# One kernel on one core: the first 166 words of a hand-written issue order replaced by 164 others

## Chip, cores and metric

One core of a Trainium2 chip runs the whole program. The metric is the device time of one execution in microseconds. Lower is better. The profile is that of one execution; engines are named PE (matrix products), DVE, ACT and POOL (element-wise work) and SP (whose queue only issues DMAs here; ACT's queue issues a few as well).

## What is computed

A conditioned block: six vectors come from `silu(c) @ w_mod`, and a linear attention and a gated MLP with a product over the positions are each put behind a layer norm that these vectors scale and shift.

```python
mod = (_silu(c) @ w_mod).reshape(1, 6, 1, 448)
sa, ca, ga, sb, cb, gb = ...
h = _layernorm(x) * (1 + ca) + sa
x = x + ga * A(h)          # q, k, v = h @ wqkv; 16 heads of 28
                           # phi_q, phi_k = [softmax(p), softmax(-p)] with p = q @ w_phi, k @ w_phi
                           # o = phi_q @ (phi_k^T v) / (phi_q . sum phi_k); o @ wo
h = _layernorm(x) * (1 + cb) + sb
x = x + gb * B(h)          # z = gelu(h @ w_in); z1 * (w_sp @ layernorm(z2) + b_sp) @ w_out
```

x is 2048 x 448, wqkv is 448 x 1344, w_sp is 2048 x 2048, all in bf16.

## The kernel before

The 2048 rows of x are 16 tiles of 128 rows. The 448 columns are four chunks of 112, so that a chunk and one row of ones (113 rows) fit the partitions; that row carries the shift of the layer norm. The program is a table, ORDER, that is read word by word. A word is a step of the function fast_path with its arguments, behind `@` the bank of the accumulator memory that it writes (`A0` to `A2` and `C` are pairs of banks), behind `/` the engine (V is DVE, S is ACT, G is POOL, Y is SP). There is no planner at run time: each engine runs its own steps in the order of the table, and a step waits for its inputs and for the bank or buffer that it overwrites. A DMA is issued in its place in the queue of SP or ACT; eight DMAs may be under way, and a ninth waits for the landing of the one whose semaphore it reuses.

The change touches the ramp, the part of the table ahead of the word `kE:4`. Its steps are these:

- `ld:` loads (L653 to L684). `wk`, `wq`, `wv` are the three parts of wqkv; `x0`, `x1` one tile of x each, `x2` two tiles, `x3`, `x4`, `x5` four each; `c`; `phi`; `wsa`, `wca`, `wsb`, `wcb`, `wmga`, `wmgb` the parts of w_mod; `wo`, `win0`, `win1` and others later.
- `du:n` (L732): n products of zeros with zeros, read by nobody.
- `ct`, `ce:1` to `ce:4` (L743 to L756): c as a column and its silu; `scb` copies it for `gr` (L938), which makes the gates ga and gb.
- `FTk`, `FTq` (L822) transpose the key and query weights on PE, in two halves; `ETk`, `ETq` (L826, L828) copy the result out. `bd` (L759) spreads w_phi into blocks. `PFk:m`, `PFq:m` (L838) fold w_phi into chunk m of the weights and `EPk`, `EPq` copy that into Wk and Wq.
- `csA`, `ccA` (L767) make the columns of sa and ca, `esA`, `ecA` (L774, L771) bring them into Ga and ca1.
- `SHk`, `SHq`, `SHv` (L781): the shift row of each weight, as a product of Ga with the unscaled weight. `SCk:m`, `SCq:m`, `SCv:m` (L799, L801) then scale chunk m; m = 0 takes its rows from the shift product.
- `l1s:i`, `l1e`, `l1r` (L845 to L853): mean and deviation of tile i; `l1a:i` (L856) writes the normalized tile to xpad. Tiles 0 to 3 are transposed to hT by PE (`X:i`, L869) and copied out by `XE:i`; later pairs go by a DMA transpose (`T1:a,b`, L861).
- `kM:i`, `vM:i` (L879, L887): k and v of tile i. `kE`, `kF` (L882) are the exponentials, `vC` (L890) the copy of v, `kS`, `kR`, `kP` (L893 to L900) the softmax normalization, `kA` (L910) the sum of phi_k^T v over the tiles. `qM`, `qE`, `qF` (L927, L932) do the same for q.
- `m1` to `m6`, `tbl`: constants, and the load of ACT's table.

In the table before, the query weights are loaded, transposed and folded first; PE makes SHv, SHk, SHq one after another, and then the products of v for tiles 0 and 1.

Of the kernel before, what the change touches and what calls it, by code (L numbers as in the profile page):

```python
# [490 lines left out]
kF:5 kE:6 l1s:14 kF:6 qM:2@A1 qE:2 qF:2 kA:0@A0 l1s:15 l1e:12,16/G l1r:12,16 l1a:14/G l1a:12/G l1a:13/G kS:3 T1:8,10 kR:3 kP:3/V kF:7 ld:wmgb/Y T1:12,14
kS:4 kR:4 l1a:15/G T1:14,16 kS:5 kR:5 kA:1@A0 kA:2@A0 kA:3@A0 vM:5@5 vC:5 vC:7 kP:4/V kP:5/G kE:7 kS:7 W:0,4 ld:win0/Y wos:1/G vC:6 kM:10@3 W:0,5 kS:6
ld:wout/Y vM:11@2 vM:4@5 vC:4 ccB@7 W:0,0 ld:bsp/Y ecB kM:9@4 kF:9 kE:9 kA:4@A0 kR:7 csB@5 esB W:0,3 kM:8@7 kF:8 kR:6 kE:8 W:0,6 kP:7/V kM:11@4 kF:11 kS:9
kS:8 kP:6/G kA:5@A0 vM:9@6 vC:9 vM:8@7 kR:8 kP:8/V kR:9 kM:12@5 kA:6@A0 kA:7@A0 kE:11 kS:11 vC:8 kF:10 kE:10 kS:10 kR:10 wos:0/G kP:9/G kR:11 kP:11/G
kP:10/V kF:12 vC:11 kE:12 kS:12 kR:12 kA:8@A0 kP:12/G kM:13@3 kF:13 vM:12@2 kM:14@4 kE:14 kF:14 kE:13 kS:13 kR:13 vC:12 vM:10@5 vC:10 kM:15@6 kF:15 kE:15
kS:14 kR:14 vM:14@7 gr:1@2 kA:9@A0 kA:10@A0 kA:11@A0 vC:14 vM:13@5 vC:13 kA:12@A0 vM:15@3 vC:15 kP:13/G kS:15 kP:14/V kR:15 kP:15/V kA:13@A0 kA:14@A0
kA:15@A0 wos:2/V ge:1 qM:3@C qE:3 KV:1 KV:0 nM:0@A1 nX:0 wts:0/V nC:0 nM:1@A2 nX:1 nC:1 nS:0 wts:1/G YB@0 YE wos:3/G nV:0 qF:3 nT:0 nA:0/G T2:0,1 SHw:2@1
SCw:0,2/S SCw:3,0/S qM:4@C qE:4 nT:1 nA:1/G SHw:3@2 SCw:0,3/V SCw:3,1/G nM:3@A2 SCw:1,1/S wts:5/V nX:3 nC:3 nM:2@A0 nX:2 nC:2 nS:1 nV:1 nT:3 nA:3/G qF:4
qM:5@A1 qE:5 qF:5 SCw:1,0/G nM:4@C nX:4 nM:5@A2 nX:5 T2:1,2 wN:1@3 SCw:2,1/S wR:1/S wQ:1/S nT:2 nA:2/V wN:0@2 wR:0/S wQ:0/S nC:4 nC:5 qM:6@A0 nS:2 nV:2
nT:5 nA:5/G SCw:0,0/V nM:6@A2 nT:4 nA:4/V nM:7@A1 lA:0,2/V lB:0,2/V T2:2,4 wN:2@7 lC:0,2/V lD:0,2/G l2r:0,2 T2:4,6 qE:6 l2a:1/G T3:1,2 nX:7 nX:6 qF:6  # L500
l2a:0/G T3:0,1 wR:2/S wQ:2/S nC:7 nC:6 nS:3 nV:3 wM:3@6 wR:3/V lA:2,4/G lB:2,4/G wQ:3/S qM:7@A0 qF:7 lC:2,4/G qE:7 lD:2,4/G l2r:2,4 l2a:3/G l2a:2/G nT:7
nT:6 nA:6/V nA:7/V T2:6,8 nM:8@A1 SCw:2,0/S T3:2,4 wM:4@6 wR:4/V W:1,1 wM:5@7 wR:5/V lA:4,6/G lB:4,6/G nM:9@A0 nX:9 nC:9 nX:8 nC:8 nS:4 nV:4 nT:8 nA:8/G
W:1,4 zM:1@A2 nT:9 nA:9/G T2:8,10 gt zG:1 zM:0@C zG:0 wM:7@3 wQ:4/S zQ:1/S wQ:5/V lC:4,6/G lD:4,6/G zA:0,2/G zB:0,2/G l2r:4,6 wM:6@2 wR:6/V wQ:6/S wR:7/V
W:1,0 zQ:0/V zC:0,2/G lA:6,8/G nM:11@A0 nX:11 nC:11 yM:0,1@5 W:0,1 yG:0,1 yM:0,0@4 wQ:7/V nM:10@A1 nX:10 nC:10 nS:5 yG:0,0 zD:0,2/G l2a:4/V l2a:5/V T3:4,6
nV:5 zM:2@C zG:2 lB:6,8/G lC:6,8/G zW:0,2 lD:6,8/G nT:11 nA:11/G zM:3@A2 zG:3 nT:10 zQ:2/S nA:10/V T2:10,12 l2r:6,8 wM:9@6 wR:9/V wM:8@7 wR:8/V l2a:6/G
nM:12@A2 nX:12 nC:12 zA:2,4/G lA:8,10/G lB:8,10/G nM:13@A1 nX:13 nC:13 nS:6 nV:6 nT:13 nA:13/V zQ:3/S yM:0,6@0 yG:0,6 yM:0,5@6 wQ:9/S l2a:7/G T3:6,8 W:0,2
W:1,2 zB:2,4/V zC:2,4/G zD:2,4/G zN:0/G yM:0,4@7 yG:0,4 wQ:8/S yG:0,5 lC:8,10/V lD:8,10/V nT:12 nA:12/G zM:4@A0 zG:4 wM:11@2 wR:11/V wQ:11/S wM:10@3
wR:10/V wQ:10/S lA:10,12/V l2r:8,10 nM:15@A2 nX:15 lB:10,12/V lC:10,12/G nM:14@A0 nX:14 lD:10,12/G l2r:10,12 zW:2,4 l2a:9/V nC:14 nC:15 nS:7 nV:7 nT:15
T2:12,14 nT:14 zN:1/V zM:5@C zG:5 nA:14/V zA:4,6/V l2a:8/G zN:2/G T3:8,10 zQ:4/S zN:3/V tT:1,2,4/V yM:0,3@3 l2a:11/G yG:0,3 W:1,6 wts:4/V l2a:10/V nA:15/V
T2:14,16 yM:1,1@2 zB:4,6/G zQ:5/S zC:4,6/G zD:4,6/G zW:4,6 T3:10,12 yM:1,3@6 yM:1,4@7 yG:1,4 zM:7@A2 zG:7 zQ:7/S yM:1,2@3 yG:1,3 zN:5/G zM:6@A0 zG:6 zQ:6/S  # L510
yM:0,2@5 yG:0,2 W:0,7 wM:13@7 yM:1,5@4 yG:1,2 yG:1,5 wR:13/V wQ:13/V zN:4/V wts:2/G zA:6,8/G zB:6,8/G zC:6,8/G zD:6,8/V zW:6,8 zN:6/G yM:1,0@1 wM:12@0
wR:12/V wQ:12/V yG:1,0 lA:12,14/V lB:12,14/G lC:12,14/G lD:12,14/V l2r:12,14 l2a:13/G l2a:12/G T3:12,14 W:1,7 zM:9@C zG:9 zQ:9/S zM:8@A2 wM:15@1 zG:8
wR:15/V wQ:15/S zQ:8/S wM:14@7 zA:8,10/V wR:14/V zB:8,10/V lA:14,16/G lB:14,16/V wQ:14/V lC:14,16/G lD:14,16/G l2r:14,16 yM:2,6@3 zM:11@A2 zG:11 zQ:11/V
yM:2,2@1 yG:2,2 zM:10@C yM:2,0@0 yG:2,6 zG:10 zQ:10/S yG:2,0 yG:1,1 zC:8,10/G tT:1,4,6/V zA:10,12/G l2a:15/V zM:12@A2 zN:7/V zG:12 l2a:14/V zB:10,12/V
T3:14,16 W:1,3 zM:13@C zD:8,10/G zW:8,10 zN:8/G zC:10,12/V zD:10,12/G yM:2,3@3 zN:9/V zW:10,12 zN:11/V zN:10/V tT:2,2,4/V zG:13 zA:12,14/V yM:1,6@1 yG:2,3
zQ:13/S zB:12,14/V zQ:12/S zC:12,14/G zD:12,14/V zW:12,14 zN:12/V zN:13/V tT:3,4,6/V tT:3,2,4/V wts:6/V tT:1,0,2/V yM:3,4@0 yG:3,4 zM:15@C zM:14@A1
yM:3,3@4 zG:15 W:1,5 sS:0,1,1/V zG:14 zA:14,16/G zQ:14/S yM:3,1@5 zB:14,16/G zQ:15/S yG:3,1 yG:1,6 zC:14,16/V zD:14,16/G zW:14,16 zN:15/V zN:14/V
tT:1,6,8/V tT:2,6,8/V yM:2,4@7 tT:2,4,6/V yG:2,4 tT:3,6,8/V yM:3,2@6 yM:3,6@0 yM:3,0@2 yG:3,0 tT:3,0,2/V tT:2,0,2/V yM:2,5@3 yM:3,5@5 yG:2,5 sS:0,1,0/V
yM:2,1@1 sS:0,2,1/V W:2,7 tT:4,2,4/V yG:2,1 tT:4,6,8/V yG:3,2 guard yG:3,5 W:2,3 W:2,4 yG:3,6 sS:0,2,0/V gM:0,6@3 W:2,2 gG:0,6 W:2,5 gM:1,6@7 sS:0,3,0/V
pM:0,0,1@6 pc:0,0 pb:0,0 pM:0,1,1@5 pM:0,0,2@6 gG:1,6 cA:0,0,11 cX:0,0,11/G tT:4,4,6/V pc:0,1 sS:0,3,1/V pM:0,2,1@1 pM:0,1,2@5 W:2,6 W:2,0 pb:0,1 pc:0,2  # L520
pM:0,2,2@1 pM:0,0,6@0 uB:0,0 pM:0,0,7@2 yG:3,3 uA:0,0 uW:0,0 pM:0,1,6@4 tT:4,0,2/G pM:0,0,4@2 pM:0,1,7@3 sS:0,4,0/V uB:0,1 uA:0,1 wts:3/V uW:0,1 pM:0,2,6@7
pb:0,2 uB:0,2 pM:0,1,4@3 cA:0,1,11 uA:0,2 pM:0,2,7@6 uW:0,2 W:3,4 W:2,1 W:3,6 W:3,0 cA:0,2,11 sS:0,4,1/V cA:0,0,21 pM:0,0,5@0 cA:0,1,21 cX:0,2,11/G
cX:0,0,21/G cX:0,1,21/G pM:0,2,4@6 W:3,7 W:3,2 W:3,5 cA:0,0,22 cX:0,0,22/V W:3,1 pM:0,1,5@4 cA:0,1,22 pM:0,0,3@0 cA:0,2,21 cX:0,2,21/V pM:0,2,5@7 cA:0,0,12
cA:0,2,22 cX:0,0,12/V cX:0,1,22/V pM:0,1,3@4 pM:0,2,3@7 sS:1,3,0/V cA:0,2,12 guard2@3 pM:1,0,1@1 pc:1,0 pM:1,1,1@2 cX:0,2,12/V cA:0,1,12 cX:0,1,12/V
sS:1,3,1/V pc:1,1 pM:1,0,2@1 cA:1,0,11 pM:1,2,1@5 pc:1,2 pM:1,1,2@2 guard3 sS:1,1,1/V sS:1,2,1/V cX:0,1,11/G cA:1,1,11 pM:1,2,2@5 oM:0,0,7@3 W:3,3
sS:1,1,0/V oE:0 oM:1,0,7@6 oE:1 oD:1/Y oD:0/Y cX:0,2,22/G pb:1,1 oM:2,0,7@0 oE:2 oM:3,0,7@4 oE:3 sS:1,2,0/V sS:1,4,0/V oM:4,0,7@3 oM:5,0,7@6 oM:6,0,7@0
# [777 lines left out]
```

## Time and profile before

| | |
|---|---|
| runs | 250.62 us median of 3 (250.29 to 251.96) |
| the profiled execution | 250.58 us, of which the span from first to last instruction is 248.7 |
| PE busy | 238.8 us of the span |
| DVE, POOL, ACT busy | 184.6, 124.9, 116.8 us |
| first product of x with a weight | 16.04 us from the start |
| granted clock of PE, mean of the span | 0.998 |

The page of the profile gives shares of the span. Views beside it list the waits (who waited for whom), the chain of work that ended last, the instructions in order of time, and, for chosen stretches, the busy time of each engine with the granted clock, the DMA share and GB/s. Times in these views count from the start of the span. A line number is that of the kernel's source.

### The profile page before, as it was taken

The page shows a single profiled execution, that of the slowest core. Times are in us where ns is not written, and L with a number is a line of the kernel's source. Part 1 is how long each engine was busy: PE and PEld are TensorE (multiplying, and loading weights), DVE is VectorE, ACT ScalarE, POOL GpSimd, SP SyncE. Part 2 cuts the span into 40 slices and gives each one's busy share as a digit, 9 for nine tenths or more (in the row PEclk, how much of TensorE's full clock was granted, in tenths as well). Part 3 has the DMA queues.
Part 4 walks back from the last instruction along what each step waited for, and adds up shares of the span by engine and source line. Part 5 has one row for each costly group of instructions (what it writes and reads, how often), then busy time and mean ns, then how long its engine had stood idle before and what let it go on. Part 6 is the DMA issues. An engine that isn't in the chain of part 4 may idle for free.

```text
span 248.7 us, 4193 instructions
## 1 busy us (share of the span) xinstructions
PE 238.8 (96%) x1511; PEld 126.3 (51%) x1519; DVE 184.6 (74%) x374; ACT 116.8 (47%) x233; POOL 124.9 (50%) x170
## 2 busy tenths in 40 slices
...
GB/s 164 263 297 165 176 242 216 190 191 0 61 68 128 171 147 150 86 129 58 108 45 4 137 158 1 3 0 151 193 35 3 37 55 55 3 0 3 18 78 67
DMA packets 68800, 25.23 MB, mean 101 GB/s; under 512 B 58401, under 2 KB 68642, under 8 KB 68770
## 3 DMA queue, kind: packets, MB, share of 16 engines
...
q8 instruction: 14, 0.23, 0.4%
...
## 4 chain that ended last, share of the span: by engine, by line
PE 90%; DMA 5%; ACT 1%; DVE 1%; issue 0%; SPq 0%; DVEq 0%
PE f_psum L1146 29%; PE f_psum L1066 10%; PE f_psum L1036 9%; PE f_psum L1095 8%; PE f_psum L927 6%; PE f_psum L1082 6%; PE f_psum L879 5%; PE f_psum L887 5%; PE f_psum L990 4%; DMA f_wv<-in_A_wqkv_dram 3%; PE f_psum L910 3%; PE f_psum L955 3%; DMA f_wq_raw<-in_A_wqkv_dram 2%; PE f_psum L781 1%; ACT f_Eq L932 1%; PE f_psum L786 1%
## 5 line engine op out<-in xcount | busy, mean ns | idle before, releaser
L1146 PEld LDWEIGHTS <-f_z2n 128*128 128x128 bf16 x192 | 18.7, 98 | 22.4
L1146 PE MATMUL f_psum<-f_wsp,f_z2n 128*128 128x512 bf16 x119 | 27.2, 379 | 0.1
L1198 POOL TENSOR_TENSOR f_z1T<-f_gb,f_z1T 128x512 bf16<-128x512 f32 x6 | 8.4, 1414 | 35.8 <-DVE f_gb L1173 35.8
L1036 PE MATMUL f_psum<-f_win,f_hT 112*128 112x448 bf16 (+1 forms) x128 | 26.2, 352 | 0.0
L1066 PE MATMUL f_psum<-f_hT,f_win 112*128 112x512 bf16 x112 | 26.0, 379 | 0.0
L1146 PE MATMUL f_psum<-f_hT,f_Eq 128*128 128x512 bf16 x92 | 22.3, 379 | 0.2
L1166 ACT COPY f_Eq<-f_psum 128x512 f32<-128x512 f32 x4 | 2.3, 586 | 38.6 <-PE f_psum L1146 38.6
L1095 PE MATMUL f_psum<-f_wout,f_z1T 128*128 128x448 bf16 x105 | 20.4, 352 | 0.0
L1069 ACT ACTIVATE f_z1T<-f_psum,f_yb 128x512 bf16<-128x512 f32 x28 | 18.1, 682 | 1.8 <-PE f_psum L1066 1.8
L1036 PEld LDWEIGHTS <-f_hT 112*128 112x128 bf16 (+1 forms) x128 | 12.3, 97 | 11.7
L932 ACT ACTIVATE f_Eq<-f_psum 112x1024 bf16<-112x1024 f32 x16 | 16.1, 1033 | 3.7 <-PE f_psum L927 3.5
L893 DVE TENSOR_REDUCE f_ksum<-f_E 128x32 f32<-128x896 bf16 x16 | 16.7, 1062 | 1.5 <-ACT f_E L882 1.5
L974 DVE TENSOR_TENSOR f_t<-f_psum,f_w 128x896 bf16<-128x896 f32 x16 | 16.9, 1086 | 0.5
L1066 PEld LDWEIGHTS <-f_win 112*128 112x128 bf16 x112 | 10.9, 98 | 12.3
L882 ACT ACTIVATE f_E<-f_psum 128x448 bf16<-128x448 f32 x32 | 15.7, 567 | 2.8 <-PE f_psum L879 2.2
L1040 ACT ACTIVATE f_z2g<-f_psum 128x896 bf16<-128x896 f32 x16 | 14.6, 914 | 4.8 <-PE f_psum L1036 4.0
L900 POOL TENSOR_TENSOR f_phik<-f_E,f_kr 128x896 bf16<-128x896 bf16 x8 | 14.5, 1813 | 4.5 <-DVE f_kr L897 3.8
L1111 DVE TENSOR_TENSOR f_xpad<-f_psum,f_x 128x448 bf16<-128x448 f32 x15 | 9.2, 621 | 8.6 <-PE f_psum L1095 8.6
L1146 PEld LDWEIGHTS <-f_Eq 128*128 128x128 bf16 x96 | 9.4, 98 | 11.3
L927 PE MATMUL f_psum<-f_hT,f_Wq 113*128 113x512 bf16 (+1 forms) x64 | 15.0, 378 | 0.0
L1095 PEld LDWEIGHTS <-f_z1T 128*128 128x128 bf16 x105 | 10.2, 98 | 9.4
L887 PE MATMUL f_psum<-f_wv,f_hT 113*128 113x448 bf16 (+1 forms) x64 | 14.1, 352 | 0.0
...
## 6 DMA issues: line engine op xcount, KB each, us to landing
...
f_wm<-in_w_mod_dram SPq DMA_DIRECT2D x4, 406.0 KB, 6.6
f_win<-in_B_w_in_dram SPq DMA_DIRECT2D x2, 784.0 KB, 6.6
f_x<-in_A_x_dram SPq DMA_DIRECT2D x3, 448.0 KB, 9.5
f_wmg<-in_w_mod_dram SPq DMA_DIRECT2D x2, 392.0 KB, 7.2
f_wout<-in_B_w_out_dram SPq DMA_DIRECT2D x1, 784.0 KB, 9.4
...
f_wq_raw<-in_A_wqkv_dram ACTq DMA_DIRECT2D x1, 392.0 KB, 4.8
```

Source lines behind the costliest of these rows:

```text
L882: nc.scalar.activation(out=Er[i % NR][:, s, :], in_=ps["k" + str(i)][:, 0, 0:D], func=ACT.Exp, scale=1.0 - 2.0 * s)
L887: nc.tensor.matmul(t[:, 0, 0:D], lhsT=hT[0:KR[m], i, m, :], rhs=wv[0:KR[m], m, :], start=(m == 0), stop=(m == KC - 1))
L893: nc.vector.tensor_reduce(out=ksum[:, i], in_=Er[i % NR][:].rearrange("p s (c f h) -> p (s c) h f", c=4, h=HP), axis=AX.X, op=ALU.add)
L927: nc.tensor.matmul(t[:, u, :], lhsT=Wq[0:KR[m], m, cc * CB:cc * CB + P], rhs=hT[0:KR[m], 4 * st:4 * st + 4, m, :], start=(m == 0), stop=(m ...
L932: nc.scalar.activation(out=Eq[st // 2][0:CB, 2 * c2:2 * c2 + 2, s, (st % 2) * 512:(st % 2 + 1) * 512], in_=ps["q" + str(n)][0:CB, :, :], f ...
L974: nc.vector.tensor_tensor(out=tr[i % 2][:], in0=numv(i)[:, :, :, 0:DH], in1=wr[i // 2 % 2][:, i % 2].unsqueeze(3).to_broadcast([P, 2, H, D ...
L1036: nc.tensor.matmul(t[:, hf, 0:D], lhsT=hT[0:KR[m], i, m, :], rhs=win_s[0:KR[m], m, FH + hf * D:FH + (hf + 1) * D], start=(m == 0), stop=(m ...
L1066: nc.tensor.matmul(t[:, 0, :], lhsT=win_s[0:CB, m, fc * P:(fc + 1) * P], rhs=hT[0:CB, 4 * st:4 * st + 4, m, :], start=(m == 0), stop=(m == ...
L1069: nc.scalar.activation(out=stage_b()["z1T"][:, fc, st * 512:(st + 1) * 512], in_=ps["y%d_%d" % (st, fc)][:, 0, :], func=ACT.Gelu_apprx_tan ...
L1082: nc.tensor.matmul(g[:, 0, 0:b - a], lhsT=later["z2n"][:, s_, fc * P:(fc + 1) * P], rhs=wspT[t][:, s_, a:b], start=(s_ == 0), stop=(s_ == ...
L1095: nc.tensor.matmul(ps["o" + str(t)][:, 0, 0:D], lhsT=later["z1T"][:, fc, t * P:(t + 1) * P], rhs=wout_s[:, fc, :], start=(fc == 0), stop=( ...
L1146: nc.tensor.matmul(t[:, 0, :], lhsT=b[:, j, f * P:(f + 1) * P], rhs=a[:, j, :], start=(PSTART[k] and j == 0), stop=(j == NH - 1), skip_gro ...
```

## The change

Only the table is edited. From `kE:4` on, its 811 words are the same in the same order (they are wrapped into other lines). Ahead of that:

- wk comes by ACT's queue and wq by SP's; x0 is ahead of x1; x2 is behind wsa and wca; wmga and wcb are ahead of x5; wo is behind `T1:4,6`.
- The key weights are transposed and folded ahead of the query weights.
- SHk and SHq are ahead of SHv; the products of k for tiles 0 and 1 are ahead of those of v.
- 18 products of zeros instead of 24, all at the start.
- Banks are given out anew, and some copies and scalings change their engine.

```diff
-ld:x1/Y m2b/G m5 m1/V du:3@1 du:3@5 du:3@7 du:3@3 du:3@0 ld:wq/S ld:c/S tbl m2a/G ld:wk/Y ld:phi/Y l1s:1 bd/V l1e:1,2/G l1r:1,2 ld:x0/Y l1s:0 l1e:0,1/G m4
-FTq:0@5 ETq:0/S ct@1 ce:1 FTq:1@3 ETq:1/V FTk:0@7 ETk:0/S l1r:0,1 l1a:0/G FTk:1@6 ETk:1/S ce:2 ce:3 ce:4 scb du:3@0 m3 du:3@2 ld:x2/Y PFq:3@3 PFq:1@7
-EPq:1/S du:3@0 ld:wsa/Y PFq:0@4 m6 l1a:1/V X:1@0 PFq:2@1 l1s:2 l1s:3 l1e:2,4/V l1r:2,4 EPq:0/S PFk:0@5 EPk:0/S csA@6 esA PFk:1@2 EPq:3/S PFk:2@7 EPk:2/V
-EPk:1/S PFk:3@4 EPk:3/S X:0@5 XE:0/V ld:wca/Y ccA@6 ecA EPq:2/S ld:wv/Y SHv@3 SCv:1/S SCv:0/S SCv:2/V SHk@7 SCk:0/S SCk:1/S SHq@6 XE:1/V l1a:2/G X:2@0
-XE:2/S ld:x3/Y l1a:3/G X:3@4 SCk:2/V SCv:3/V vM:0@5 XE:3/S vM:1@1 SCk:3/V vC:1 SCq:3/S vC:0 kM:0@7 vM:2@0 vC:2 kE:0 kF:0 kM:1@2 kM:2@5 ld:x4/Y SCq:2/S
-SCq:1/V ld:wo/Y ld:x5/Y SCq:0/S l1s:5 l1s:4 l1s:7 kM:3@4 ld:wcb/Y kF:1 l1s:6 l1e:4,8/V l1r:4,8 l1a:7/G kF:2 l1a:6/G vM:3@7 vC:3 kE:1 kE:2 kF:3 l1s:9 l1s:11
-kE:3 l1s:8 l1a:5/G qM:0@A0 l1s:10 l1a:4/V qE:0 l1e:8,12/G l1r:8,12 l1a:11/G qM:1@A1 qE:1 l1s:13 l1s:12 qF:1 kS:0 ld:wmga/Y gr:0@5 kS:1 T1:6,8 vM:6@6 vM:7@4
-kM:7@7 ge:0 qF:0 kR:0 l1a:9/G kR:1 l1a:8/G l1a:10/G T1:4,6 kM:4@2 kP:1/G kP:0/V
+m5 m1/V ld:wk/S m2a/G m2b/G du:3@3 du:3@1 du:3@2 du:3@4 ld:x0/Y l1s:0 l1e:0,1/G du:3@5 du:3@7 ld:c/S ct@3 FTk:0@6 tbl ce:1 ce:2 ce:3 ce:4 scb FTk:1@2
+l1r:0,1 l1a:0/G m3 ld:wq/Y FTq:0@3 ld:x1/Y FTq:1@0 ETk:0/V ld:phi/Y ld:wsa/Y bd/V ETk:1/S PFk:1@6 PFk:3@7 PFk:0@1 ETq:1/V ETq:0/S EPk:3/S PFk:2@4 X:0@3
+EPk:0/S EPk:1/V PFq:3@0 EPq:3/S EPk:2/S PFq:2@5 l1s:1 l1e:1,2/G csA@7 esA PFq:1@1 EPq:1/S EPq:2/V PFq:0@2 EPq:0/S ld:wca/Y ccA@6 ld:x2/Y XE:0/S l1r:1,2
+SHk@0 ecA SCk:1/S SCk:0/S l1s:2 SCk:2/V l1s:3 l1a:1/G m4 SCk:3/V l1e:2,4/G l1r:2,4 ld:wv/Y SHq@5 SCq:1/V X:1@7 XE:1/S SCq:2/V ld:x3/Y SHv@3 SCv:2/S SCv:0/S
+SCv:1/V SCv:3/V SCq:0/S kM:0@2 kF:0 l1s:4 kM:1@0 kF:1 l1s:5 l1s:6 l1s:7 vM:1@3 l1a:3/G X:3@7 XE:3/S kE:0 SCq:3/S kS:0 l1a:2/G vM:0@4 X:2@6 XE:2/S kE:1 vC:0
+vC:1 kM:3@5 kF:3 kE:3 l1e:4,8/G l1r:4,8 l1a:6/G vM:3@1 vC:3 l1a:4/G ld:x4/Y l1s:8 kM:2@6 l1a:5/G l1a:7/V m6 l1s:9 ld:wmga/Y gr:0@0 l1s:10 l1s:11 l1e:8,12/G
+l1r:8,12 l1a:9/G l1a:11/G l1a:8/G kR:0 kF:2 ld:wcb/Y ld:x5/Y l1s:12 vM:2@7 qM:1@A2 vC:2 ge:0 qM:0@A1 qF:1 kE:2 qE:1 T1:6,8 kM:7@7 vM:6@6 qF:0 T1:4,6 kM:4@1
+kP:0/V kS:1 l1s:13 vM:7@4 kR:1 ld:wo/Y l1a:10/V qE:0 kP:1/G
 kE:4 ld:win1/Y kS:2 kR:2 kF:4 T1:10,12 kM:5@0 kE:5 ld:wsb/Y kP:2/G kM:6@5
...
```

More of the change, by code (lines that the diff above doesn't have):

```diff
@@ L491 @@
[L491 to L526, printed above, removed]
```

50 lines of the change are left out of this document (43 added, 7 removed).

## The prediction, as it went on record

> **What bounds the kernel now.** I read the page first. Its first two lines say who works:
>
> ```profile
> span 248.7 us, 4193 instructions
> PE 238.8 (96%) x1511; PEld 126.3 (51%) x1519; DVE 184.6 (74%) x374; ACT 116.8 (47%) x233; POOL 124.9 (50%) x170
> ```
>
> PE is the bound; only its late start can be won. So the next view is the chain that ended last, over the first 31 us (start, length, what):
>
> ```profile
> 0.72 4.83 DMA f_wq_raw<-in_A_wqkv_dram
> 5.55 0.02 issue
> 5.57 0.32 SPq L660
> 5.89 0.04 issue
> 5.93 7.33 DMA f_wv<-in_A_wqkv_dram
> 13.26 0.04 issue
> 13.30 2.44 PE f_psum L781 x12
> ```
>
> Until 13.26 the chain is DMA: the value weights wv land then. From 13.30 on it is PE: first the three shift products SHv, SHk, SHq (L781, four matmuls each, 2.44 us together), then two transposed tiles (X:2, X:3) and the products of x. PE's waits (who waited for whom, total, times, longest), in 13.2 to 60 us and in 60 to 70 us:
>
> ```profile
> PE f_psum L781 <- DMA f_wv<-in_A_wqkv_dram: 0.6, 1, 0.6
> ```
>
> ```profile
> PE f_psum L955 <- DVE f_t L974: 0.7, 1, 0.7
> PE f_psum L988 <- ACT f_Eq L932: 0.4, 1, 0.4
> ```
>
> The first is the wait for wv itself. So behind wv PE is not short of work for 50 us, and every microsecond of PE work that is moved from behind 13.3 to ahead of it shortens the run by one.
>
> **The change, part 1: the loads.** The words behind `kE:4` are the same. In the ramp, wk goes to ACT's queue and wq to SP's second place; x0 leads; x2 moves behind wsa and wca; wo goes from ahead of x5 to behind `T1:4,6`; wmga and wcb go ahead of x5. The issues and their times to landing (last column):
>
> ```profile
> f_wk_raw<-in_A_wqkv_dram SPq DMA_DIRECT2D x1, 392.0 KB, 5.7
> f_x<-in_A_x_dram SPq DMA_DIRECT2D x1, 224.0 KB, 5.7
> 3.18 0.47 SPq L660 DMA_DIRECT2D f_wm<-in_w_mod_dram  x1
> f_wm<-in_w_mod_dram SPq DMA_DIRECT2D x1, 406.0 KB, 7.0
> f_wm<-in_w_mod_dram SPq DMA_DIRECT2D x1, 406.0 KB, 6.2
> f_wv<-in_A_wqkv_dram SPq DMA_DIRECT2D x1, 392.0 KB, 7.3
> 3.00:21.00 18.00, 15.89 (x172) 11.05 (x171) 13.12 (x41) 12.79 (x26) 8.12 (x22) 1.00 1.12 272
> ```
>
> Landings: wq 5.55 (the chain's first row), wk 5.7 after an issue at 1.2, so 6.9, wsa 3.18+7.0 = 10.2, wca 5.57+6.2 = 11.8, wv 13.26: in order of issue, while the DMA runs full (share 1.12, 272 GB/s from 3 to 21 us). Order and bytes then set a landing. wk and wq change places: wk 5.55, wq 6.9. Ahead of wv stand the same loads as before (wk, wq, c, phi, x0, x1, wsa, wca, x2), so **wv lands at 13.26 again**, ±0.3. But wsa and wca gain the 224 KB of x2: 0.23 MB at 272 GB/s is 0.84 us, so by rate wca lands at 10.9 and wsa at 9.2 (without the gain: 11.8, 10.2), and x2 just after wca, 11.8 (at worst 12.4). The ninth load waits in both orders: SP's issue at 5.57 came with the landing of the ACT queue's first load, and now that is wk in the same place.
>
> **Part 2: the work ahead of wv.** Prices (starts of successive rows give the spacing):
>
> ```profile
> 7.12 0.63 DVE L759 TENSOR_TENSOR f_BD<-f_phi,f_bmask 112x448 bf16<-112x448 bf16 x1 [2.37 <-DMA f_phi<-in_A_w_phi_dram]
> 10.52 0.37 PE L838 MATMUL f_psum<-f_BD,f_wTq 112*112 112x112 bf16 x4
> 10.73 0.37 PE L838 MATMUL f_psum<-f_BD,f_wTk 112*112 112x112 bf16 x4
> 14.07 0.92 PE L781 MATMUL f_psum<-f_Wk,f_Ga 112*128 112x448 bf16 x4
> 14.83 0.92 PE L781 MATMUL f_psum<-f_Wq,f_Ga 112*128 112x448 bf16 x4
> 15.83 0.62 DVE L845 BATCH_NORM_STATS2 f_st<-f_x 128x6 f32<-128x448 bf16 x1
> 21.70 1.35 SPq L861 DMA_TRANSPOSE f_hT<-f_xpad  x1
> 16.10:24.60 8.50, 7.93 (x18) 1.00 0.86 194
> ```
>
> A fold group costs PE 0.21, a shift product 0.76; the last row (ACT alone) gives 7.93/18 = 0.44 for one ACT operation; the rows of 15.83 and 21.70 are the start of the statistics of tiles 4 to 7 and the issue of T1:6,8. Walking the new order: wk at 5.55, so `ct`, `FTk` at 5.6 to 7.0; `FTq` waits for wq and for bank 3, which `ce:4` frees, 7.2 to 8.1. `bd` is behind `ETk:0` on DVE, done at 8.3; the four `PFk` then take 0.84, to 9.2; `X:0`, `PFq:3`, `PFq:2` to 9.8; `csA` (wsa is there) to 10.2; `PFq:1`, `PFq:0` to 10.7; `ccA` waits for wca, 10.9 to 11.4. ACT copies behind them one at a time, the last (`EPq:0`) at 11.6. So **SHk runs at 11.4 and SHq at 12.1, to 12.9, ahead of wv**; `X:1` fits to 13.1. At 13.3 only SHv is left. Before, SHv was followed by SHk, SHq and two X; now by two X, further down. Gain: 2 x 0.76 = **1.52 us**. If wca gains nothing (11.8), SHk and SHq end at 13.7 and PE is 0.4 late: gain 1.1. If `PFk` came a further 1.5 us late as well: gain 0. The other way, wv 0.3 early with SHq done in time: 1.8.
>
> The dummies fall from 24 matmuls to 18. They cost nothing before 13.3 and save nothing; what they keep up is the clock:
>
> ```profile
> 1.23 3.38 PE L732 MATMUL f_psum<-f_zero 128*128 128x256 bf16 x15 [1.23 <-DVE f_zero L693]
> 5.00:6.00 1.00, 0.41 (x8) 0.41 (x8) 0.00 (x0) 0.00 (x0) 0.86 (x3) 1.00 1.19 249
> 244.00:245.00 1.00, 0.02 (x1) 0.00 (x0) 0.39 (x1) 0.00 (x0) 0.00 (x0) 1.00 0.59 183
> 247.60:248.70 1.10, 0.00 (x0) 0.00 (x0) 0.00 (x0) 0.00 (x0) 0.00 (x0) 0.51 0.05 15
> ```
>
> The first 15 took 3.38 us, so 18 end at 5.3. The granted clock stayed 1.00 in a microsecond with PE 41% busy, and fell to 0.51 at 247.6, some 3.5 us after PE's last matmul at 244.0. My walk has no gap of PE over 0.5 us (5.3 to 5.6, 10.7 to 10.9), so I cost the lost dummies at nothing; without that cover, one stretch as long as that, 3.5 us, at half pace costs 1.7. The Trainium skill, TensorE: Matmul & The Clock Gate, Part 1, speaks against taking fillers out: the clock returns to half after an idle window of about 3.4 us, in windows that run freely. The fall at 247.6 agrees with it; by that rule too the gaps here are too short, and the sum is unchanged.
>
> **Part 3: from 13.3 to where the orders meet.** PE has the same products in both (8 of k and v, `gr:0`, two qM). New order: SHv to 14.06, `kM:0`, `kM:1`, `vM:1`, `X:3`, `vM:0`, `X:2`, `kM:3`, `vM:3`, `kM:2`, `gr:0`, `vM:2`, `qM:1`, `qM:0`. Each needs ACT to be in time. With 0.45 to 0.55 for each of ACT's operations, SCv:0 is done at 15.4 (`vM:1` asks at 15.6), XE:3 at 17.35 (`kM:3` at 17.5), XE:2 at 18.85 (`kM:2` at 19.05), kE:3 at 21.1 (`qM:1` at 21.35). All fit, with 0.15 to 0.25 to spare, and late hand-overs share one ACT backlog instead of adding up. DVE has l1s:2 and l1s:3 ahead of SCk:3, which is then done at 13.9 (with x2 at 12.4: 14.5, wanted at 14.6). The statistics of tiles 4 to 7 follow at 14.9; with the old 5.9 us from there T1:6,8 is issued at 20.8, which leaves it 4.0 us to land for `kM:7` at 24.8. I take the whole 1.5 here; the lower bound is a 10% slower ACT over these 13 us, 1.3 us, which leaves 0.2. Above zero nothing more can come, since PE is full.
>
> **Part 4: behind the meeting point.** The moved loads can bite here:
>
> ```profile
> 9.47 1.72 SPq L669 DMA_DIRECT2D f_x<-in_A_x_dram  x1
> f_x<-in_A_x_dram SPq DMA_DIRECT2D x1, 448.0 KB, 11.5
> 24.46 0.58 SPq L653 DMA_DIRECT2D f_win<-in_B_w_in_dram  x1
> f_win<-in_B_w_in_dram SPq DMA_DIRECT2D x1, 784.0 KB, 6.9
> 27.02 1.23 SPq L861 DMA_TRANSPOSE f_hT<-f_xpad  x1
> f_hT<-f_xpad SPq DMA_TRANSPOSE x1, 5.6
> 21.00:23.00 2.00, 2.00 (x12) 0.96 (x11) 1.90 (x6) 2.00 (x6) 1.83 (x4) 1.00 0.22 54
> 24.00:27.00 3.00, 3.00 (x17) 1.44 (x15) 3.00 (x6) 2.93 (x5) 2.89 (x6) 1.00 0.77 134
> 35.07 0.93 PE L879 MATMUL f_psum<-f_Wk,f_hT 113*128 113x448 bf16 x4
> ```
>
> x5 landed at 21.0; with wmga and wcb (798 KB) in place of wo (392) ahead of it, 0.42 MB at 272 GB/s, it lands at 22.5. DVE reaches `l1s:12` at 22.4, so no more than some tenths are lost there, with `kP:0`, `kS:1`, `kR:1` and `l1a:10` behind it. `l1a:10` releases T1:10,12: 26.3 instead of 27.0. wo is now between T1:4,6 and win1, so T1:10,12 is behind 0.40 MB more: 1.5 us at 272 GB/s, less the 0.7 by which it and win1 start earlier. Its landing is not told; the queue puts it between win1 (24.46+6.9 = 31.4) and the next transpose (the row of 5.6, issued 1.9 us after T1:10,12, so 34.5). It is next behind win1, so I take 31.7. `kM:10` reads it at 35.07, in the new order at 33.5. Landing near 32.5 costs nothing; at the late bound (34.5+0.8) it costs 1.8, the gain and a little. I take nothing. Everything later waits for progress and not for a clock time, and moves by the same 1.5.
>
> **Sum.** The profiled execution took 250.58 us (span 248.7 and 1.9 around it), the median of the runs is 250.62. 250.58 - 1.5 = **249.1 us**, own range 248.5 to 249.8.
>
> **Rivals.**
> *Hand-overs eat the gain* (wca no earlier, or ACT the bound from 14 to 27 us): gain 0 to 0.7, 249.9 to 250.6. For it: ACT is busy for 7.93 of 8.5 us, and the margins are 0.15 to 0.25. Against: behind 13.3 ACT has seven scalings and hT copies instead of nine, since SCk:0 and SCk:1 now run ahead of wv. Chance 0.17.
>
> *Slower: tiles 10 and 11 of hT arrive late.* The place is `kM:10`, where PE stands with all that is behind it. It decides from a landing of 35.0 on (33.5 and the gain of 1.5). If wo moves at the 134 GB/s of 24 to 27 us, its 0.40 MB takes 3.0 us: from the late bound 34.5 + 3.0 - 0.7 = 36.8, a stall of 3.3, 252.4. T1:8,10 and two more follow in the same queue; each late pair adds up to an equal step, so 251 to 255, with 253 in the middle. For it: wo, win1 and four transposes now stand in one queue in 23 to 35 us, and that stretch moved only half the full rate. Against: the DMA had room just before (share 0.22 in 21 to 23), and the first taken value, 31.7, leaves a microsecond. Chance 0.20, of which 0.11 beyond 253.1.
>
> *The clock falls to half in the ramp.* 1.7 us of PE time goes: 250.8. The clock's rows speak against. Chance 0.03.
>
> *More than the shift:* wv lands 0.3 early, and PE's two waits of 60 to 70 us (0.7 and 0.4) close because ACT and DVE arrive ahead: 250.58 - 1.5 - 0.3 - 1.1 = 247.7. Nothing shows that these waits would close. Chance 0.10.
>
> **How the numbers follow.** The forecast holds 0.50. About 1% (2.5 us) is what a measurement of this kernel can tell from no change. Faster by over 1% (below 248.1) needs the last rival: 0.10. Slower by over 1% (above 253.1) is the larger half of the slow rival: 0.11. The rest, 0.79, is within. The range is 247.9 to 252.9, with 0.08 left out below and 0.12 above.
>
> **What would show it.** In the new profile: SHk and SHq (L781 on f_Wk, f_Wq) start before 13.0, SHv at 13.3, the first k product near 14.1; wca's issue to landing ends near 11; the first products of the common part (`kM:5`) 1.5 us earlier than now; no wait of PE over 0.5 between 14 and 56 us. Wrong if SHk starts after 12.5, if wv lands outside 13.0 to 13.6, if PE waits at `kM:10`, or if the granted clock drops between 6 and 14 us.

## The result, and the profile after

The kernel after took 248.19 us (median of 4 runs, 248.08 to 248.21), the kernel before, run beside it, 250.55 (4 runs, 250.29 to 251.96): a ratio of 0.99, 95% interval 0.9864 to 0.9935. The profiled execution took 248.18. The forecast was 249.1, so the gain is 2.4 us where 1.5 was foreseen: inside the range on record (247.9 to 252.9), outside the sum's own range (248.5 to 249.8). Three executions stand outside the ratios as slow: one of the kernel before with 510.46 us, and 253.76 in x_head and 253.82 in x_shv, which are counted in those two runs' medians.

The page's first two lines:

```profile
span 246.4 us, 4186 instructions
PE 238.6 (97%) x1505; PEld 126.3 (51%) x1513; DVE 184.2 (75%) x371; ACT 115.5 (47%) x232; POOL 125.1 (51%) x174
```

The stretch of 3 to 21 us in the view of windows (PE, PEld, DVE, ACT, POOL busy; clock, DMA share, GB/s):

```profile
3.00:21.00 18.00, 17.82 (x176) 12.07 (x175) 14.46 (x41) 14.19 (x31) 11.28 (x26) 1.00 0.95 252
```

PE has the same work, less the six products of zeros, in a span 2.3 us shorter. In 3 to 21 us it is now busy for 17.82 of 18 us instead of 15.89. The instructions in order of time, from the issue of wv to the first product of x:

```profile
5.25 0.47 SPq L653 DMA_DIRECT2D f_wv<-in_A_wqkv_dram  x1
...
11.02 0.92 PE L781 MATMUL f_psum<-f_Wk,f_Ga 112*128 112x448 bf16 x4
11.77 0.92 PE L781 MATMUL f_psum<-f_Wq,f_Ga 112*128 112x448 bf16 x4
...
12.75 0.92 PE L781 MATMUL f_psum<-f_wv,f_Ga 112*128 112x448 bf16 x4
...
13.51 0.74 PE L879 MATMUL f_psum<-f_Wk,f_hT 113*128 113x448 bf16 x3
```

And wv's row among the DMA issues (last column, issue to landing):

```profile
f_wv<-in_A_wqkv_dram SPq DMA_DIRECT2D x1, 392.0 KB, 6.6
```

SHk and SHq run at 11.02 and 11.77, ahead of wv. wv lands at 5.25 + 6.6, in the finer times of the trace 11.88, and not at 13.26. SHv starts at 12.75, when PE is through with what stands ahead of it. The chain of work that ended last says the same: no load of weights is in it. It begins with the load of tile 0, goes from POOL to PE and, in the first 31 us, stays there.

```profile
8.36 0.72 POOL f_xpad L856
...
11.15 1.54 PE f_psum L781 x8
...
12.91 0.76 PE f_psum L781 x4
13.67 1.52 PE f_psum L879 x8
```

How the shift is carried to the end is seen in two groups of products, the first behind the place where the orders meet (L910) and the last of all (L1100), with first and last start in us. Before:

```profile
L910 PE MATMUL f_psum<-f_vaug,f_phik x128: 212/214/224, 32.7 to 54.6; 128*128 128x116 bf16 x128
...
L1100 PE MATMUL f_psum<-f_wout,f_z1T x14: 259/259/259, 242.5 to 243.8; 128*128 128x224 bf16 x14
```

After:

```profile
L910 PE MATMUL f_psum<-f_vaug,f_phik x128: 212/214/225, 30.6 to 52.5; 128*128 128x116 bf16 x128
...
L1100 PE MATMUL f_psum<-f_wout,f_z1T x14: 259/259/259, 240.4 to 241.7; 128*128 128x224 bf16 x14
```

Both groups are earlier by nearly the same (32.65 to 30.58, 2.07, and 242.52 to 240.42, 2.10). The other 0.3 between the two executions lies behind the last product: 4.92 us from its start to the end of the span before and 4.72 now, and 1.90 against 1.80 outside the span. Over all the profiles that tail is 4.57 to 4.92, so no run shows that the edit shortens it. The two waits of PE at 60 to 70 us are there as before; in 13.2 to 60 us PE waits for nothing:

```profile
PE f_psum L955 <- DVE f_t L974: 0.7, 1, 0.7
PE f_psum L988 <- ACT f_Eq L932: 0.4, 1, 0.4
```

So 2.07 has two parts. SHk and SHq ahead of wv: 1.52. SHv at 12.75 and not at 13.30: 0.55.

### The profile page after: what moved, and what is told of

Read it like the earlier page. It is cut to its first block, busy times and chain, and to the rows that moved or that the text cites. A ratio compares the mean times of both kernels' runs of the same rounds, so it can differ in the third digit from the quotient of the medians.

```text
span 246.4 us, 4186 instructions
## 1 busy us (share of the span) xinstructions
PE 238.6 (97%) x1505; PEld 126.3 (51%) x1513; DVE 184.2 (75%) x371; ACT 115.5 (47%) x232; POOL 125.1 (51%) x174
## 4 chain that ended last, share of the span: by engine, by line
PE 92%; DVE 1%; ACT 1%; issue 1%; POOL 1%; DMA 1%; DVEq 0%; POOLq 0%
PE f_psum L1146 29%; PE f_psum L1066 10%; PE f_psum L1036 9%; PE f_psum L1095 8%; PE f_psum L927 6%; PE f_psum L1082 6%; PE f_psum L879 5%; PE f_psum L887 5%; PE f_psum L990 4%; PE f_psum L910 3%; PE f_psum L955 3%; DMA f_x<-in_A_x_dram 1%; PE f_psum L781 1%; ACT f_Eq L932 1%; PE f_psum L786 1%
## 5 line engine op out<-in xcount | busy, mean ns | idle before, releaser
L882 ACT ACTIVATE f_E<-f_psum 128x448 bf16<-128x448 f32 x32 | 16.2, 565 | 2.7 <-PE f_psum L879 2.7
L1095 PEld LDWEIGHTS <-f_z1T 128*128 128x128 bf16 x105 | 10.2, 98 | 9.4
```

What stands on the lines that cost most here:

```text
L882: nc.scalar.activation(out=Er[i % NR][:, s, :], in_=ps["k" + str(i)][:, 0, 0:D], func=ACT.Exp, scale=1.0 - 2.0 * s)
L1095: nc.tensor.matmul(ps["o" + str(t)][:, 0, 0:D], lhsT=later["z1T"][:, fc, t * P:(t + 1) * P], rhs=wout_s[:, fc, :], start=(fc == 0), stop=( ...
```

## The experiments

They ask three things: which part of the edit makes the 1.52, what the 0.55 is, and whether zeros and wo were rightly costed at nothing. One rule, found on the way, reads them all: in each profiled execution the first product of L1100 starts 209.8 to 209.9 us behind the first of L910 (x_wo 210.1; x_du0, which met a late transfer, 210.8), so what happens in the ramp decides the time, but for the tail of 4.57 to 4.92.

### r_before and r_after: both kernels once more

> The kernel before once more, unchanged, for its landings. Theory L (the order of the loads sets how fast they come): wv lands at 13.0 to 13.5 again, the loads run at 265 to 272 GB/s, time 250.3 to 250.7. Theory R (the pace of the first loads differs from execution to execution, whatever the order): wv may land anywhere from 11.9 to 13.4, and the time follows it.

> The changed kernel once more, unchanged. Theory L: wv lands at 11.7 to 12.1, SHv starts at 12.7 to 12.8, 248.0 to 248.3. Theory R: wv lands between 11.9 and 13.4; up to 12.7 the time does not notice, beyond it the time grows by the rest, to 248.8.

r_before: 250.99 us (8 runs), 1.0027 [0.9997, 1.0056] of the kernel before beside it. r_after: 248.14 (5 runs), 0.9909 [0.9872, 0.9947]. wv landed at 13.30 and at 11.98, as in the first pair, so the landing looked like a property of the order; r_after2 and x_bdu below undo that. New in r_before was the clock. Windows of its profile:

```profile
4.09:7.50 3.41, 2.30 (x33) 1.81 (x32) 0.88 (x3) 0.98 (x2) 1.01 (x3) 1.00 1.16 255
7.50:10.92 3.42, 3.42 (x30) 2.98 (x28) 3.31 (x9) 2.23 (x3) 1.99 (x7) 0.50 1.13 256
```

The first column is the window, the third from the end the granted clock. The clock was granted at 4.09, fell to half at 7.50 and came back at 10.92, in steps of 3.41 us. In the window ahead of the fall PE was busy for 2.30 of 3.41 us: it stood for 1.0 us until the query weights had landed at 5.38. PE reached SHv at 13.38 there, just behind wv, and did not wait for it.

### x_loads and x_head: the loads or the work alone

x_loads is the kernel before with the loads ahead of `kE:4` in the order of after; x_head is the kernel after with the first ten loads in the order of before.

```diff
x_loads (order of the first loads; all other words as before)
-x1/Y wq/S c/S wk/Y phi/Y x0/Y x2/Y wsa/Y wca/Y wv/Y ... wo/Y x5/Y wcb/Y wmga/Y
+x0/Y wk/S wq/Y c/S x1/Y phi/Y wsa/Y wca/Y x2/Y wv/Y ... wmga/Y wcb/Y x5/Y wo/Y
x_head (order of the first ten loads; all other words as after)
-wk/S x0/Y c/S wq/Y x1/Y phi/Y wsa/Y wca/Y x2/Y wv/Y
+x1/Y wq/S c/S wk/Y phi/Y x0/Y x2/Y wsa/Y wca/Y wv/Y
```

> The work of before with the loads of after (queues and order), nothing else. Theory L: wv lands near 11.9 as in the changed kernel. Theory R: as it comes. In both the PE order is the old one: its query weights come second now (6.2 or later instead of 5.6), the work ahead of SHv ends no earlier than 12.6, so SHv starts at 12.6 to 13.3 and the gain over before is 0 to 0.7: 249.9 to 250.6. A rival that gives the loads the whole gain says 248.2 to 248.6.

> The work of after with the first ten loads in the order of before (wq on ACT's queue; x1, wk, phi, x0, x2, wsa, wca, wv on SP's). wk lands at 6.9 and x0 at 7.4 instead of 4.8 and 3.4, so X:0 waits for x0, about 2 us more, and all PE work behind it with it: SHk at 12.5 to 13, SHv at 14.2 to 14.8, 249.6 to 250.3: half or more of the gain lost. Theory L: wv lands at 13.0 to 13.5; theory R: as it comes. A rival that gives the work order the whole gain says 248.2 to 248.6.

x_loads: 252.11 us (10 runs), 1.0068 [1.0042, 1.0094]: slower. x_head: 250.76 (10 runs), 1.0024 [0.9982, 1.0066]. Neither half alone gains. In x_loads wv was there at 12.53, but PE was not:

```profile
6.92 1.00 PE L822 MATMUL f_psum<-f_ident,f_wq_raw 112*112 112x112 bf16 x8 [2.30 <-DMA f_wq_raw<-in_A_wqkv_dram]
...
10.59 1.49 PE L732 MATMUL f_psum<-f_zero 128*128 128x256 bf16 x6
...
16.03 0.92 PE L781 MATMUL f_psum<-f_wv,f_Ga 112*128 112x448 bf16 x4
```

The work begins with the query weights, which come second in this order: PE stands for 2.30 us, and then runs at half pace until 13.81 (six products of zeros in 1.49 us, where 15 took 3.38 on the cold start of before). In x_head the key weights come second, and PE waits 0.8 for them (the view of waits):

```profile
PE f_psum L822 <- DMA f_wk_raw<-in_A_wqkv_dram: 0.8, 1, 0.8
```

The clock came at 9.99, SHv at 14.52, where wv had landed at 12.45. Three of the ten runs, 253.11 to 253.76, list a mean granted clock of 0.976 or 0.977, the others 0.989 and more; none of the three was profiled. In both halves PE waits for the weights that it folds first, and the clock comes late: they have to be those that are loaded first.

### x_wv: the landing of the forecast, made

```diff
-ld:wv/Y SHq@5 SCq:1/V X:1@7 XE:1/S SCq:2/V ld:x3/Y SHv@3
+SHq@5 SCq:1/V X:1@7 XE:1/S SCq:2/V ld:x3/Y ld:wv/Y SHv@3
```

> The kernel after, with the load of wv one place later, behind x3. Theory A (PE is full from 7.9 us on, and the end follows the start of the first k product one for one): wv lands at 13.1 to 13.4, as in the kernel before, PE waits 0.3 to 0.6 for it ahead of SHv, kM:0 starts at 13.9 to 14.1, and the time is 248.6 to 248.8, which is the forecast's 249.1 less 0.2 to 0.5. Rival B (the ACT hand-overs behind SHv have slack that absorbs half a microsecond): 248.2 in spite of the wait. Rival C (the loads' pace is set by this kernel's work, not by the order): wv lands by 12.7, no wait, 248.2.

249.19 us (10 runs, 248.52 to 249.55), 0.9946 [0.9923, 0.9969]. wv landed at 13.55, and PE waited 1.17 for it. A row of the order in time, and the group of L910:

```profile
13.60 0.93 PE L781 MATMUL f_psum<-f_wv,f_Ga 112*128 112x448 bf16 x4 [1.17 <-DMA f_wv<-in_A_wqkv_dram]
```

```profile
L910 PE MATMUL f_psum<-f_vaug,f_phik x128: 212/214/225, 31.4 to 53.4; 128*128 128x116 bf16 x128
```

Theory A expected the wait; it was longer than the 0.3 to 0.6 it gave, since PE was early here, and the time is above its 248.6 to 248.8. SHv is 0.30 later than in the kernel before, L910 is 1.21 earlier (32.65 to 31.44): 1.21 + 0.30 = 1.51, the shift of 1.52 without the early wv. SHv is 0.85 later than in the profile of after, L910 and L1100 0.86, so rival B falls, and with the landing of 13.55 rival C. (The whole execution is 1.03 longer; the rest is the tail, 4.88 against 4.72.) With wv 0.3 later than the forecast had it, the kernel takes 249.19, close to the forecast's 249.1.

### x_shv: SHv first again

```diff
-SHk@0 ecA ... ld:wv/Y SHq@5 ... SHv@3
+SHv@3 SHk@0 ecA ... SHq@5 ...        (ld:wv/Y right behind ld:x2/Y)
```

> The kernel after, with SHv ahead of SHk and SHq, and everything else in place. Theory A: PE, in order, stands from 11.0 to the landing of wv at 11.9, 0.85 to 0.9 us, then does the three shift products; kM:0 starts at 14.3 to 14.5 instead of 13.5, and the time is 249.0 to 249.2. Rival B (the hand-overs set the pace further on and give part of it back): 248.3 to 248.7. Rival C (the order of the shift products is worth its whole 1.52): 249.7.

252.16 us (10 runs, 249.86 to 253.82), 1.0031 [0.9996, 1.0065]. All three expectations were too low. The shift products in order of time, and two windows:

```profile
12.90 0.96 PE L781 MATMUL f_psum<-f_wv,f_Ga 112*128 112x448 bf16 x4 [1.79 <-DMA f_wv<-in_A_wqkv_dram]
13.66 1.70 PE L781 MATMUL f_psum<-f_Wk,f_Ga 112*128 112x448 bf16 x4
```

```profile
10.24:13.65 3.41, 1.62 (x28) 1.14 (x26) 1.57 (x5) 1.79 (x5) 1.89 (x7) 1.00 1.11 296
13.65:17.07 3.42, 3.42 (x14) 1.64 (x12) 1.94 (x8) 1.30 (x2) 0.72 (x3) 0.50 1.12 284
```

wv landed at 12.77 with the same loads ahead of it as in after, so PE stood for 1.79. That left it busy for 1.62 us of the window from 10.24 to 13.65, and the clock fell to half for the next one: SHk and SHq take 1.70 as drawn (the length in the row; neighbours overlap) instead of 0.92, and the first product of x starts at 17.07 where 12.90 + 3 x 0.76 + 0.22 (X:1) = 15.40 was due. A window at half pace costs 1.67 us here; the prediction had put 1.7 on it. The Trainium skill, TensorE: Matmul & The Clock Gate, Part 1, says that the activity window is 3.4 us and free-running, which the steps of 3.41 us, at another place in each execution, show; it asks for an idle window before the clock falls, and here a window with PE at work for 1.62 us, in r_before one with 2.30, was idle enough. The measurement decides.

### x_wo: wo back ahead of x5

```diff
-ld:wcb/Y ld:x5/Y ... kR:1 ld:wo/Y
+ld:wcb/Y ld:wo/Y ld:x5/Y ... kR:1
```

> The kernel after, with the load of wo back ahead of x5 (behind wcb), so that it is out of the queue between T1:4,6 and win1. Theory A: x5 lands at 21.7 to 22.2 instead of 20.5, T1:10,12 is issued 0.6 to 1.0 earlier, kM:10 waits for nothing in either kernel, and the time is 248.1 to 248.4. Rival B (the statistics of tile 12 wait for x5 and what is queued behind them on DVE comes late): 248.6 to 249.4. Rival C (the late wo cost something that no wait shows): 247.6 to 247.9.

248.25 us (4 runs), 0.9897 [0.9849, 0.9944]: the same as after. x5 landed at 22.25, where after has 11.56 + 8.9 = 20.46, and no wait of PE came of it. After, in order of time (the issues of x5 and of T1:10,12, and `kM:10`), and x5's row among the DMA issues:

```profile
11.56 0.49 SPq L669 DMA_DIRECT2D f_x<-in_A_x_dram  x1
...
25.68 1.23 SPq L861 DMA_TRANSPOSE f_hT<-f_xpad  x1
...
33.00 0.92 PE L879 MATMUL f_psum<-f_Wk,f_hT 113*128 113x448 bf16 x4
```

```profile
f_x<-in_A_x_dram SPq DMA_DIRECT2D x1, 448.0 KB, 8.9
```

T1:10,12 in x_wo:

```profile
25.89 1.23 SPq L861 DMA_TRANSPOSE f_hT<-f_xpad  x1
```

Theory A's time held; its detail did not: T1:10,12 was not issued earlier without wo ahead of it, but 0.2 later, so it waits for its rows and not for the queue. What wo does to the queue shows one transpose later: T1:8,10, issued at 27.64 in after and 27.84 in x_wo, landed at 34.92 and at 33.31, and no product waited for it.

### x_du0: no products of zeros

```diff
-du:3@3 du:3@1 du:3@2 du:3@4 ... du:3@5 du:3@7
```

> The kernel after, without its 18 products of zeros. Theory A (the clock is granted after some microseconds of dense PE work, and without the zeros that work starts only with c and wk at 4.8): the grant comes at 10 to 13 us instead of 6.5, some 25 to 30 fold and transposing groups run at twice their price, kM:0 starts 1.0 to 2.5 us late, and the time is 249.2 to 250.7. Rival B (the loads and ACT bound the ramp anyway, and the zeros are idle weight): wait for nothing new, 248.1 to 248.5.

250.17 us (10 runs), 0.9968 [0.9938, 0.9999]. PE in order of time, a window and a wait:

```profile
5.27 1.74 PE L822 MATMUL f_psum<-f_ident,f_wk_raw 112*112 112x112 bf16 x16
...
8.41 1.70 PE L838 MATMUL f_psum<-f_BD,f_wTk 112*112 112x112 bf16 x16
...
12.50 0.92 PE L781 MATMUL f_psum<-f_Wk,f_Ga 112*128 112x448 bf16 x4
```

```profile
4.97:8.39 3.42, 3.42 (x36) 3.35 (x36) 1.75 (x5) 1.51 (x3) 2.20 (x4) 1.00 1.15 256
```

```profile
PE f_psum L990 <- DMA f_oo<-f_oo: 0.9, 1, 0.9
```

The 16 fold products of the key weights take 1.70 instead of 1.09 as drawn, SHk is 1.48 later than in after, and the clock is granted at 11.80 instead of 6.47. The time is in theory A's range, but dense work alone did not bring the clock: the window from 4.97 to 8.39 was full of small products (3.42 us busy), and the grant came a window later. A further 0.9 of this profile is a wait for a transfer at 75 us that no other profile has. The 18 zeros are worth some 1.5 us (SHk) to 2 us (the medians), an estimate; that the six which the edit drops cost nothing fits with PE's 17.82 busy us of 18, but was not tried by itself.

### r_after2: the landing of wv once more

> The kernel after once more, for the pace of its loads and its scatter. Theory A (the landing of wv scatters by some 0.9 us between executions, but is before 12.75, where PE is ready for SHv): wv lands anywhere in 11.8 to 12.8, SHv starts at 12.7 to 12.9 all the same, and the time is 248.0 to 248.4. Rival (the order of the loads fixes the landing): 11.8 to 12.1 for the third time.

248.24 us (7 runs, 247.74 to 248.95), 0.9913 [0.988, 0.9946]; the profiled one took 248.62. The issue of wv and SHv in order of time, wv's row among the DMA issues, and the group of L910:

```profile
5.62 0.47 SPq L653 DMA_DIRECT2D f_wv<-in_A_wqkv_dram  x1
...
13.20 0.93 PE L781 MATMUL f_psum<-f_wv,f_Ga 112*128 112x448 bf16 x4
```

```profile
f_wv<-in_A_wqkv_dram SPq DMA_DIRECT2D x1, 392.0 KB, 7.5
```

```profile
L910 PE MATMUL f_psum<-f_vaug,f_phik x128: 212/214/225, 31.0 to 53.0; 128*128 128x116 bf16 x128
```

The same program, and wv lands at 13.15, 1.27 later than in the first profile; the whole of the ramp's loads ran slower. It is outside both expectations, and with it falls the reading that the order fixes the landing. In this profile wv, and not PE, sets SHv by some 0.1 us. SHv at 13.20 is 0.10 earlier than in the kernel before, L910 1.62 (32.65 to 31.03): again 1.51 and the difference of SHv.

### x_bdu: the gap of the kernel before filled

```diff
+du:5@0 FTq:0@5
-FTq:0@5
```

> The kernel before, with five more products of zeros ahead of the transposes of the query weights, in the stretch of 4.6 to 5.6 us in which PE waits for wq. Theory A (the scatter of the kernel before, 249.1 to 251.9, is the clock: a window of 3.4 us that holds this gap is not granted the full rate, or loses it, and where the windows lie differs from run to run): with the gap filled no window is too thin, the cluster of runs at 251.3 to 251.9 is gone, and the runs lie in 249.1 to 251.0; the median, which such a run hardly moves, is 250.0 to 250.5. Theory B (the scatter is the pace of the loads, wv landing at 12.4 to 14.6 by chance): the runs scatter as before, up to 251.9. In the profiled run wv lands at 13.2 to 13.4 if the order of the loads fixes it, anywhere in 12.4 to 13.4 if chance does.

249.7 us (12 runs, 249.32 to 252.65), 1.0001 [0.9973, 1.0028]: no difference that shows. Ten of the runs lie in 249.32 to 250.57, two at 251.30 and 252.65, so theory A's claim that all runs then lie below 251.0 is not borne out. What the cluster is comes up again behind the table below. SHv in order of time, and the group of L910:

```profile
12.46 0.93 PE L781 MATMUL f_psum<-f_wv,f_Ga 112*128 112x448 bf16 x4
```

```profile
L910 PE MATMUL f_psum<-f_vaug,f_phik x128: 211/214/224, 31.8 to 53.8; 128*128 128x116 bf16 x128
```

With the load words of the kernel before, wv landed at 12.41, and everything behind it is 0.84 earlier, at SHv as at L910. PE stood 0.11 us for wv. So here, as in the profile of before, SHv goes with the landing of wv, and that is not fixed by the load words.

### x_bsh: one shift product moved alone

```diff
-SHv@3 SCv:1/S SCv:0/S SCv:2/V SHk@7 SCk:0/S
+SHk@7 SHv@3 SCv:1/S SCv:0/S SCv:2/V SCk:0/S
```

> The kernel before, with SHk ahead of SHv and nothing else moved. Theory A (PE, once it has work, is full from the shift products on, so the end stands at a fixed distance behind the first product of x; the key weights are folded only at 13.0 here, so one product of 0.76 is ahead of wv for 0.3 at most): where wv lands at 13.2 to 13.4, SHk starts at 13.0, PE's wait for wv goes, the first product of x starts at 15.7 instead of 16.0, and the run takes 250.2 to 250.4; where wv lands by 12.5, SHk's place costs up to 0.4, since PE then waits for the key weights with wv there. Median 250.0 to 250.6, no difference that shows. Rival B (the swap alone is worth the product it moves): the first product of x at 15.3, 249.7 and less. On the loads: wv at 13.2 to 13.4 for the third time in this order would speak for the order of the loads, a landing by 12.6 for chance.

250.43 us (12 runs), 1.0005 [0.998, 1.003]: no difference, as theory A said. Its numbers missed: PE was late here, SHk came at 13.68 and not at 13.0, behind wv (12.93); the clock came only at 10.38. L910 is 18.58 behind SHv, one product of 0.76 less than in the kernel before. Swapping the product without folding the key weights first gains nothing.

### x_best1: an attempt to go further

```diff
-PFk:0@1 ... X:0@3 EPk:0/S ... PFq:2@5          (scb behind ce:4, ld:phi behind ld:x1)
+PFk:0@1 ... EPk:0/S ... PFq:2@5 X:0@3          (scb behind l1a:0/G, ld:phi ahead of ld:x1)
```

> The kernel after, with X:0 two fold groups later (behind PFq:2), the load of phi ahead of x1, and the copy of the silu columns behind the normalized tile 0 on POOL. Theory A (from 7.9 us on PE sets SHv, and wv has 0.8 us to spare): the fold begins at 7.7 instead of 7.87 and the 0.34 that PE waits for tile 0 goes, SHv starts at 12.2 to 12.5, and the time is 247.7 to 248.0. Rival B (the columns of ca wait for wca, or SHv for wv, wherever the loads run slower): no gain, 248.1 to 248.4.

247.92 us (6 runs, 247.64 to 248.5), 0.9914 [0.9884, 0.9944], against 0.9913 for r_after2 on the same chip: not told apart from after. PE in order of time:

```profile
7.92 1.26 PE L838 MATMUL f_psum<-f_BD,f_wTk 112*112 112x112 bf16 x16
...
12.72 0.92 PE L781 MATMUL f_psum<-f_wv,f_Ga 112*128 112x448 bf16 x4
```

PE no longer waits for POOL, but the clock was granted 0.5 later in this profile (6.96), the fold began at 7.92, and SHv gained 0.03.

## The landing of wv and the time, over the profiles

| profile | wv landed | SHv starts | first L910 | time of that execution |
|---|---|---|---|---|
| before | 13.26 | 13.30 | 32.65 | 250.58 |
| r_before | 13.30 | 13.38 | 32.72 | 250.18 |
| x_bdu (work and loads of before) | 12.41 | 12.46 | 31.81 | 249.53 |
| after | 11.88 | 12.75 | 30.58 | 248.18 |
| r_after | 11.98 | 12.78 | 30.61 | 248.27 |
| r_after2 | 13.15 | 13.20 | 31.03 | 248.62 |
| x_wv (work of after) | 13.55 | 13.60 | 31.44 | 249.21 |

In all profiles with the work of before (x_loads too) L910 is 19.33 to 19.35 behind SHv; in all with the work of after, but for x_shv, 17.82 to 17.84, and in x_bsh, with one product moved, 18.58. The difference, 1.51, is the shift. SHv starts at the later of wv and PE in both kernels. In before and x_bdu that is wv; in r_before, x_bsh and x_loads, with the clock at half pace for longer, it is PE. In after, r_after, x_wo and x_best1 it is PE, at 12.63 to 12.78.

The runs of r_after and r_after2 lie from 247.7 to 249.0, those of before from 249.0 to 252.0. The landing of wv is not all of that: of 97 executions of before with a listed mean granted clock (510.46 left out), 20 took over 251.2 us, and all 20 list 0.996 or 0.997, as 14 of the other 77 do. So this cluster goes with the clock. None of it was profiled, so how it comes about stays open. In x_bdu none of the 12 runs is over 251.2 with these values, beside it 3 of 20 of before; that is too few to say that filling the gap did it.

## Why the prediction was right, and where not

**Part 2, the work ahead of wv:** held. SHk and SHq came at 11.02 and 11.77 (11.4 and 12.1 foreseen), X:1 fits behind them, and the gain of 1.52 is in every profile, whenever wv landed (19.34 against 17.83).

**Part 1, the loads:** "wv lands at 13.26 again", with 0.3 either way, is the step that failed. One execution's landing was taken for a fixed value; the same words gave 11.88, 11.98 and 13.15 in after, and 13.26, 13.30, 12.41 (x_bdu) and 12.93 (x_bsh) in the order of before. By the prediction's own sign (a landing outside 13.0 to 13.6) it was wrong here. This mis-sized term is the 0.55 of SHv. The other loads came early too in the first profile: wsa 8.33 for 9.2 (10.2 less 0.84 is 9.3), wca 9.76 for 10.9.

The 0.55 looks like luck more than like the order. Over the seven profiles with the first ten loads in the order of after, wv landed at 11.88 to 13.15, mean 12.47; over the five with the order of before at 12.41 to 13.30, mean 12.87. The pace differs before the orders do: both begin with 392 KB on ACT's queue and one tile of x on SP's, and those 392 KB landed at 4.79 in after and 5.55 in before. At a like landing of these (5.14 to 5.15), wv came at 12.77 and 13.15 in the new order (x_shv, r_after2) and at 12.45 in the old (x_head). Twelve profiles leave open whether some tenths belong to the order. The medians of three pairs differ by 2.36, 2.32 and 2.13 us, more than 1.52, which speaks for something beyond the shift; part of that can be the cluster of before that goes with the clock, and what share it has stays open.

**The clock:** the walk's claim that no gap is long enough held for after. But the reason given, gaps under 3.5 us do no harm, was wrong: 1.79 us of standing was enough in x_shv, and in x_loads PE ran at half pace until 13.81 behind a wait of 2.30. The price of 1.7 for a window at half pace was right, the condition was not. The microsecond it read for this, 5.00 to 6.00 in before, could not show it: the clock is settled by windows of 3.41 us, here 5.28 to 8.69 with PE busy for 3.01, and what lies ahead of the first grant at 5.28 is listed as 1.00 in any case. Taking out all the zeros is not free either (x_du0).

**Part 3, the hand-overs:** held. No wait in 13.2 to 60 us, so that rival was worth nothing.

**Part 4, behind the meeting point:** held, with a margin. x5 came at 20.46 and not 22.5, `kM:10` ran at 33.00 without a wait (T1:10,12, the next in the queue, had been issued at 25.68), and x_wo shows that wo's new place is worth nothing either way in the time. The delay that the slower rival named is there (T1:8,10 landed 1.6 later than in x_wo), but no product waited for it.

**More than the shift:** half of it came true. wv was early, by more than the rival said, and the two waits of 60 to 70 us stayed. The time of 248.18 in the profile is 1.52 of shift, 0.55 of an early wv, and 0.3 behind the last product that nobody foresaw.
